# Seven-product layer: combinations kept in PSUM, products reordered, six weight chunks converted in layer 1, one GpSimd piece per tick

## The chip, the core and the metric

The kernel runs on one core of a Trainium2 chip. The metric is the device time of one execution in microseconds (us); lower is better. Engines are named as in the profile: PE (matmul), DVE (VectorE), ACT (ScalarE), POOL (GpSimd) and SP (the queue that issues DMAs).

## The reference

x has the shape 2 x 3008 x 256 in float32, so there are 6016 tokens of 256 numbers.

```python
X = np.fft.fft(np.fft.fft(x, axis=1), axis=2).real        # 2 x 3008 x 256
x = X.reshape(6016, 256)
h = x @ w_in                                              # 256 -> 2048
g = np.where(h > 0, h, np.exp(np.minimum(h, 0)) - 1)      # ELU
x = g @ w_out                                             # 2048 -> 256
h = x @ w2_in                                             # 256 -> 2048
g = np.maximum(h, 0) + alpha * np.minimum(h, 0)           # PReLU, alpha per column
return g @ w2_out                                         # 2048 -> 256
```

## The kernel before

**Arithmetic.** All matrix products are in float32r. An operand is split into hi (rounded by a copy on ACT) and lo = value - hi (a subtraction on POOL, sometimes on DVE), and a product is three matmuls: hi x hi, lo x hi, hi x lo (`PASSES`). The 6016 tokens lie in six blocks, each of two column sets of 512, 512, 480, 484, 512 and 512 tokens (`BLOCKS`). 2048 hidden columns are 16 tiles of 128 (`NFT`).

**Layer 1: 96 ticks.** `tick(t)` is one hidden tile of one block. Blocks 0 and 1 are interleaved in halves, the others run one after another; ticks 64 to 79 are block 4 and ticks 80 to 95 block 5. In a tick PE does gemm1 of t (6 matmuls, L413, into the two PSUM banks of the tag `mm`) and gemm2 of t-3 (12 matmuls, L429, into four accumulator banks `acc`). DVE forms pt and two ht from gemm1 (L546 to L548), ACT does relu and exp, DVE combines the ELU of t-1 (L515), ACT writes hi of t-2 (L525) and POOL lo of t-2 (two pieces, L531). gemm2 therefore waits for lo, and lo for hi. From tick 42 on (`E_PSUM`) the exp goes into the two PSUM banks of the tag `ee`.

**Side work in the ticks.** Hooks `pre`, `mid` and `end` of each tick carry work for layer 2. Its weights are stored as 64-bit numbers and are converted in halves of 512 columns: one ACT copy (`conv_y`, L307) and three integer steps on DVE (`conv_s`: L324, L326, L328). `KEEP` lists the chunks (("i" or "o", layer, chunk), tick of its load, of its first step, of its return) that are converted in layer 1 and parked in DRAM; `DIRECT` lists those converted in layer 2. For an "i" chunk `sums` makes sums of weight quarters and `split_sx` their hi and lo. `FINAL_1` splits parked chunks at ticks 84 to 94. `PREP_0` prepares block 0 for layer 2: `sub` makes differences of quarters (t3, t1, t2, t4; L484), `cast` their hi (ACT, L375) and lo (L376). When a block of layer 1 ends, `evac` copies its accumulators (DVE, L449, the first two, ACT the others).

**Layer 2: 48 pairs.** `pair(p)` does two hidden tiles of one block for both column sets, eight pairs for each block, by seven products of the Strassen kind in place of eight. A product is 3 matmuls (`product`, L602) with a weight quarter or sum (A11, A12, A22, S1 to S4) and a prepared operand (b11, t1, ...). They run into four PSUM banks: a and b of the tag `mm`, d and e of `ee`. Three banks take two products (a: A11 + A12, d: S1 + S4, e: S3 + A22), b takes S2. After them, `second(p-1)` does the 24 matmuls of gemm2 of the pair before (L429). The combinations are

```python
v  = A11 + S2          # P1 + P6            (L656, DVE)
h0 = d + v             # second column set  (L666, DVE)
h1 = (e + v, S1 + S3 + v)                 # (L668 and L652, L669, DVE)
```

with a itself the fourth. ACT does a relu of each (L665, L667, L670), DVE the PReLU (L673), ACT hi (`hi_2`, L620, 1024 wide, one for each hidden tile) and POOL lo (`lo_2`, L626, four pieces) for gemm2 in the next pair. In pairs 0 to 8 the rows of `FIRST` (one for each pair: what goes at its start, and after its products) carry the remaining weight conversion and the preparation of block 1; `AHEAD` carries the preparation of the later blocks. At the pair after a block ends (9, 17, 25, 33, 41) ACT and DVE also evacuate four accumulators.

The order on every engine is the order in which the code issues instructions (`manual_schedule`); each engine goes through its own in order.

Of the kernel before, what the change touches and what calls it, by code (L numbers as in the profile page):

```python
# [100 lines left out]
def tile_fft_moe_elu_moe_prelu(  # L101
# [254 lines left out]
    def w_split(kind, layer, c, i):  # L356
# [10 lines left out]
        act(out=hi, in_=v, func=ACTF.Copy)  # L367
        nc.gpsimd.tensor_tensor(out=lo, in0=v, in1=hi.bitcast(F32), op=ALU.subtract)


    sx = []
    s3 = {}

    def hi_lo(hi, lo, v, eng):
        act(out=hi, in_=v, func=ACTF.Copy)  # L375
        eng.tensor_tensor(out=lo, in0=v, in1=hi.bitcast(F32), op=ALU.subtract)  # L376

    def sums(c, eng, ks=(0, 1, 2, 3)):
# [4 lines left out]
        s = s3[c]
        ops = [(s[:, 1], w[:, 0, 0], w[:, 0, 1], ALU.subtract), (w[:, 0, 1], w[:, 0, 1], w[:, 1, 1], ALU.add),
               (s[:, 0], w[:, 0, 1], w[:, 0, 0], ALU.subtract), (s[:, 2], w[:, 1, 0], s[:, 0], ALU.subtract)]
        for k in ks:
            o, a, b, op = ops[k]
            eng.tensor_tensor(out=o, in0=a, in1=b, op=op)

    def split_sx(c, i):  # L390
# [87 lines left out]
    def sub(bl, name, eng=nc.vector):  # L478
# [5 lines left out]
        eng.tensor_tensor(out=o, in0=a, in1=b, op=ALU.subtract)  # L484
# [12 lines left out]
    def cast(bl, name, eng="g"):  # L497
# [131 lines left out]
    def pair(p, pre, mid, end):  # L629
        for fn in pre:  # L630
            fn()
        if p - 1 in pr:
            lo_2(p - 1, 0)
        if p < NP:
            bl, j = divmod(p, NFT // 2)
            n = BLOCKS[bl][2]
# [12 lines left out]
        if p < NP:
            e = tile_("ee")  # L650
            product(p, S3, "t3", e, True, False)
            tt(out=h1[:, 1], in0=e[:, 0:n], in1=h1[:, 1], op=ALU.add)  # L652
# [4 lines left out]
            product(p, A12, "b21", a, False, True)
            product(p, S4, "b22", d, False, True)
            product(p, A22, "t4", e, False, True)
        for fn in mid:  # L660
# [50 lines left out]
    with tc.manual_schedule():  # L711
# [54 lines left out]
        for bl, t in LOAD_ZB.items():  # L766
            at(t, load_zb, bl)
        for key, t_ld, t0, t_get in KEEP:
            at(t_ld, load, key)
# [8 lines left out]
            at(t_get, fetch_w, key)
        for t, kind, c, i in FINAL_1:
            at_split(t, kind, 2, c, i)  # L780
        for key, t in DIRECT.items():
            (at if t else at2)(t, load, key)

        def conv3(kind, c, i):
            for step in range(3):
# [9 lines left out]
            "sums": lambda c: sums(c, nc.vector),  # L795
            "sx": lambda c: [split_sx(c, i) for i in range(3)],
        }
        for p, (pre, mid) in enumerate(FIRST):
            for what, *args in pre + mid:
                where = "pre" if (what, *args) in pre else "mid"  # L800
                if p == 0:
                    at(NT - 1, does[what], *args, where="end")
                else:
                    at2(p - 1, does[what], *args, where=where)
# [5 lines left out]
        at(PREP_0[0], load_xs, 0, where="mid")  # L810
        for i, name in enumerate(("t3", "t1", "b11", "t2", "t4", "b21", "b22")):
            t = PREP_0[i + 1]
            if name[0] == "t":
                at(t, sub, 0, name, nc.gpsimd, where="end")
            if name != "t4":
                at(t + 1, cast, 0, name, where="mid")
        at(PREP_0[7] + 2, cast, 0, "t4", where="mid")
# [90 lines left out]
```

## Time and profile before

| | before |
|---|---|
| median of 3 runs | 985.65 us (985.25 to 987.08) |
| the profiled execution | 987.81 us |
| its span in the trace | 986.0 us |
| granted TensorE clock, mean over the span | 0.997 |
| PE busy | 955.3 us |
| DVE, ACT, POOL busy | 757.0, 650.9, 653.8 us |

The profiled execution is 1.81 us longer than its span and 2.16 us longer than the median. Layer 1's ticks 64 to 95 run from 341.00 to 479.44 us, layer 2's pairs from 479.44 us to the end.

### The profile page before, as it was taken

The page shows a single profiled execution, that of the slowest core. Times are in us where ns is not written, and L with a number is a line of the kernel's source. Part 1 is how long each engine was busy: PE and PEld are TensorE (multiplying, and loading weights), DVE is VectorE, ACT ScalarE, POOL GpSimd, SP SyncE. Part 2 cuts the span into 40 slices and gives each one's busy share as a digit, 9 for nine tenths or more (in the row PEclk, how much of TensorE's full clock was granted, in tenths as well). Part 3 has the DMA queues.
Part 4 walks back from the last instruction along what each step waited for, and adds up shares of the span by engine and source line. Part 5 has one row for each costly group of instructions (what it writes and reads, how often), then busy time and mean ns, then how long its engine had stood idle before and what let it go on. Part 6 is the DMA issues. An engine that isn't in the chain of part 4 may idle for free.

```text
span 986.0 us, 12143 instructions
## 1 busy us (share of the span) xinstructions
PE 955.3 (97%) x4206; PEld 770.0 (78%) x4206; DVE 757.0 (77%) x1002; ACT 650.9 (66%) x877; POOL 653.8 (66%) x492
## 2 busy tenths in 40 slices
PE   9799989999999999999999999999999999999998
PEld 3576757788888877778777778888888888888886
DVE  2797989989999989777899986676767576757554
ACT  5577776766788887788766655656555556556554
POOL 1365667766867867878777966666675675666553
PEclk9999999999999999999999999999999999999999
DMA  8963322201211311021230020002002002001001
GB/s 317 331 203 85 86 76 86 96 21 66 76 51 54 118 62 53 2 85 43 86 129 1 0 83 1 1 1 84 1 0 83 1 1 84 1 1 43 1 1 43
DMA packets 27109, 63.04 MB, mean 64 GB/s; under 512 B 3044, under 2 KB 12516, under 8 KB 25000
## 3 DMA queue, kind: packets, MB, share of 16 engines
q1 hardware_dynamic: 25632, 61.03, 18.9%
q10 hardware_dynamic: 1160, 1.07, 0.4%
q8 instruction: 33, 0.54, 0.2%
q0 software_dynamic: 256, 0.17, 0.1%
q14 instruction: 28, 0.23, 0.1%
HBM read 40.99 MB, written 21.27 MB: 63 GB/s over the span
## 4 chain that ended last, share of the span: by engine, by line
PE 73%; DVE 14%; ACT 5%; issue 3%; POOL 3%; DMA 2%; DVEq 0%; ACTq 0%; SPq 0%; POOLq 0%
PE acc L429 40%; PE eet L602 11%; PE mmt L602 8%; PE mmt L413 6%; POOL lo L531 2%; DVE pt L546 2%; DVE ht L548 2%; DVE et L673 2%; DVE et L518 1%; PE eet L182 1%; PE eet L413 1%; ACT et L565 1%; DVE sg L326 1%; ACT hi L525 1%; PE mmt L182 1%
## 5 line engine op out<-in xcount | busy, mean ns | idle before, releaser
L429 PE MATMUL acc<-hi,wo 128*128 128x512 f32 (+2 forms) x1536 | 470.9, 388 | 4.3 <-ACT hi L525 2.4
L626 POOL TENSOR_TENSOR lo<-et,hi 128x512 fp32r<-128x512 f32 (+2 forms) x190 | 255.3, 1367 | 160.6 <-ACT hi L620 154.9
L429 PEld LDWEIGHTS acc<-hi,wo 128*128 128x128 f32 x1536 | 289.1, 188 | 61.5 <-ACT hi L525 3.3
L531 POOL TENSOR_TENSOR lo<-et,hi 128x512 fp32r<-128x512 f32 (+2 forms) x192 | 268.8, 1424 | 93.9 <-ACT hi L525 62.3
L429 PE MATMUL acc<-lo,wo 128*128 128x512 f32 (+2 forms) x768 | 299.1, 390 | 9.5 <-POOL lo L531 9.5
L429 PEld LDWEIGHTS acc<-lo,wo 128*128 128x128 f32 x768 | 144.8, 189 | 43.8 <-POOL lo L531 16.0
L565 ACT ACTIVATE et<-ht 128x1024 f32<-128x1024 f32 (+3 forms) x97 | 100.2, 1033 | 87.4 <-DVE ht L548 76.8
L413 PE MATMUL mmt<-zt,wi 128*128 128x512 f32 (+2 forms) x462 | 121.1, 395 | 1.8 <-ACT zt L273 0.8
L652 DVE TENSOR_TENSOR ht<-eet,ht 128x512 f32<-128x512 f32 (+2 forms) x48 | 32.6, 679 | 113.9 <-ACT ht L645 113.9
L620 ACT ACTIVATE hi<-et 128x1024 fp32r<-128x1024 f32 (+2 forms) x96 | 99.9, 1040 | 23.6 <-DVE et L673 22.0
L673 DVE SCALAR_TENSOR_TENSOR et<-et,oma_sb,ht 128x512 f32<-128x512 f32 (+2 forms) x96 | 110.4, 1189 | 0.0
L413 PEld LDWEIGHTS mmt<-zt,wi 128*128 128x128 f32 x462 | 86.8, 189 | 23.3 <-issue 3.0
L525 ACT ACTIVATE hi<-et 128x1024 fp32r<-128x1024 f32 (+3 forms) x97 | 99.1, 1022 | 3.0 <-DVE et L518 2.5
L546 DVE SCALAR_TENSOR_TENSOR pt<-zb,an_sb,mmt 128x512 f32<-128x512 f32 (+2 forms) x77 | 56.2, 730 | 29.6 <-PE mmt L413 29.4
L641 ACT ACTIVATE p<-mmt 128x512 f32<-128x512 f32 (+2 forms) x48 | 28.3, 589 | 74.6 <-PE mmt L602 74.6
L670 ACT ACTIVATE et<-ht 128x1024 f32<-128x1024 f32 (+2 forms) x48 | 50.2, 1046 | 40.7 <-DVE ht L669 40.6
L518 DVE SCALAR_TENSOR_TENSOR et<-et,ht 128x1024 f32<-128x1024 f32 (+2 forms) x44 | 66.8, 1521 | 1.8 <-POOL lo L531 1.1
L602 PE MATMUL eet<-xo,wi 128*128 128x512 f32 (+2 forms) x216 | 60.8, 390 | 7.0 <-DVE ht L652 7.0
L515 DVE SCALAR_TENSOR_TENSOR et<-eet,ht 128x512 f32<-128x512 f32 (+2 forms) x106 | 66.5, 669 | 0.0
L602 PE MATMUL mmt<-xo,wi 128*128 128x512 f32 (+2 forms) x216 | 60.1, 386 | 0.9 <-ACT p L641 0.9
L572 ACT ACTIVATE eet<-et 128x512 f32<-128x512 f32 (+2 forms) x106 | 58.4, 584 | 3.4 <-DVE et L515 1.8
L602 PE MATMUL eet<-xo,sx 128*128 128x512 f32 (+2 forms) x216 | 60.0, 386 | 0.0
(125 smaller groups left out, 1330.0 us busy)
## 6 DMA issues: line engine op xcount, KB each, us to landing
w<-w_in SPq DMA_DIRECT2D x8, 1024.0 KB, 5.3
w<-w_out SPq DMA_DIRECT2D x8, 1024.0 KB, 8.0
vt<-ud SPq DMA_DIRECT2D x6, 1024.0 KB, 4.7
ud<-uc SPq DMA_DIRECT2D x20, 256.0 KB, 4.3
xd<-xs SPq DMA_DIRECT2D x8, 512.0 KB, 3.5
xs<-xd SPq DMA_DIRECT2D x4, 1024.0 KB, 10.6
out_t<-ot SPq DMA_DIRECT2D x16, 256.0 KB, 2.2
xc<-x SPq DMA_DIRECT2D x5, 768.0 KB, 7.9
```

What stands on the lines that cost most here:

```text
L413: mm(out=p[:, 0:n], lhsT=lhsT, rhs=rhs, start=(i == 0), stop=(i == len(ops) - 1))
L429: mm(out=accs[L, bl][d][t][:, 0:n], lhsT=w[:, a, o, d * 128:(d + 1) * 128], rhs=(hi, lo)[b][:, t, 0:n], start=(f == first and i == 0), sto ...
L515: stt(out=s["e"][:, i, :], in0=s["x"][i], scalar=-1.0, in1=s["h"][:, i, :], op0=ALU.add, op1=ALU.max)
L518: stt(out=s["e"][:, i], in0=s["e"][:, i], scalar=-1.0, in1=s["h"][:, i], op0=ALU.add, op1=ALU.max)
L525: act(out=s["hi"][:, i, 0:s["n"]], in_=s["e"][:, i], func=ACTF.Copy)
L531: nc.gpsimd.tensor_tensor(out=s["lo"][:, i, 0:n], in0=s["e"][:, i, :], in1=s["hi"][:, i, 0:n].bitcast(F32), op=ALU.subtract)
L546: stt(out=pt[:, 0:n], in0=zb[bl][:, 0:n], scalar=an_sb[:, f:f + 1], in1=p[0], op0=ALU.mult, op1=ALU.add)
L565: act(out=s["e"][:, i], in_=s["h"][:, i], func=ACTF.Relu, scale=-1.0)
L602: mm(out=bank[:, 0:n], lhsT=w[:, a], rhs=x2[b][:, 0:n], start=(first and m == 0), stop=(last and m == 2), skip_group_check=True)
L620: act(out=s["hi"][f][:, :, 0:n], in_=s["g"][f], func=ACTF.Copy)
L626: eng.tensor_tensor(out=s["lo"][f][:, t, 0:n], in0=s["g"][f][:, t], in1=s["hi"][f][:, t, 0:n].bitcast(F32), op=ALU.subtract)
L673: stt(out=o, in0=o, scalar=oma_sb[:, 2 * j + f:2 * j + f + 1], in1=h, op0=ALU.mult, op1=ALU.add)
```

## The change

**Pairs.** The products come in the order P1 (A11 into a), P6 (S2 into b), P5 (S1 into d), P7 (S3 into e), then A12, S4, A22 into a, d and e. DVE adds v = b + P1 into SBUF; all other combinations are written in place into PSUM: b = e + v, b += P5, d += v, e += v. Relu and PReLU work on the four banks singly (512 wide, one operand in PSUM). Both `hi_2` of a pair stand at its end, both `lo_2` at the start of the next.

**Weights.** `KEEP` has a sixth chunk, ("i", 2, 3); the six start every seven ticks and do their two halves in six ticks in a row. `FIRST` spreads the steps of the two chunks that stay in layer 2 as two per pair over pairs 1 to 6; the first conversion copy moves from the end of tick 95 into pair 0.

**POOL.** A helper `two` puts the hi of a split into `mid` of a tick (on ACT ahead of its relu) and the lo at the `end` on POOL, so that a tick holds at most one such piece, or one call of `sums`, beside the two of its own lo. The four `sub` of block 0 go from POOL to DVE (ticks 64, 66, 74, 78). `sub` of t3, t1 and t2 of block 1 go from DVE to POOL.

```diff
 KEEP = [
-    (("i", 2, 2), 63, 66, 95),
+    (("i", 2, 2), 59, 62, 95),
+    (("i", 2, 3), 66, 69, 98),
...
-PREP_0 = (64, 67, 70, 73, 76, 79, 82, 85)
+PREP_0 = [("x", 62), ("t3", 64, 65), ("t1", 66, 67), ("b11", None, 69), ("t2", 74, 75), ("b21", None, 76), ("t4", 78, 82),
...
 FIRST = [
-    ((("s", "o", 2, 0),), (("y", "o", 2, 1), ("w", "o", 1, 0), ("w", "o", 1, 1))),
+    ((("s", "o", 2, 0, 0), ("s", "o", 2, 0, 1)), (("y", "o", 2, 1), ("w", "i", 2, 0), ("w", "i", 2, 1))),
...
+    later = {}
+    def hi_lo(hi, lo, v, eng="g", key=None):
         act(out=hi, in_=v, func=ACTF.Copy)
-        eng.tensor_tensor(out=lo, in0=v, in1=hi.bitcast(F32), op=ALU.subtract)
+        fn = lambda: engine(eng).tensor_tensor(out=lo, in0=v, in1=hi.bitcast(F32), op=ALU.subtract)
+        if key:
+            later[key] = fn
+        else:
+            fn()
...
             lo_2(p - 1, 0)
+        if p - 1 in pr:
+            lo_2(p - 1, 1, nc.vector if p == NP else nc.gpsimd)
         if p < NP:
...
             product(p, A11, "b11", a, True, False)
             p1 = wk.tile([128, 512], F32, tag="zb", name="p1")
             act(out=p1[:, 0:n], in_=a[:, 0:n], func=ACTF.Copy)
-            h1 = wk.tile([128, 2, 512], F32, tag="h", name="ht")[:, :, 0:n]
-            d = tile_("ee")
-            product(p, S1, "t1", d, True, False)
-            act(out=h1[:, 1], in_=d[:, 0:n], func=ACTF.Copy)
-        if p - 1 in pr:
-            hi_2(p - 1, 1)
-            lo_2(p - 1, 1, nc.vector if p == NP else nc.gpsimd)
-        if p < NP:
-            e = tile_("ee")
-            product(p, S3, "t3", e, True, False)
-            tt(out=h1[:, 1], in0=e[:, 0:n], in1=h1[:, 1], op=ALU.add)
-            b = tile_("mm")
+            b = bank("mm")
             product(p, S2, "t2", b, True, True)
             v = wk.tile([128, 512], F32, tag="zb", name="v")
             tt(out=v[:, 0:n], in0=b[:, 0:n], in1=p1[:, 0:n], op=ALU.add)
+            d = bank("ee")
+            product(p, S1, "t1", d, True, False)
+            p5 = wk.tile([128, 2, 512], F32, tag="h", name="p5")[:, 0]
+            act(out=p5[:, 0:n], in_=d[:, 0:n], func=ACTF.Copy)
+            e = bank("ee")
+            product(p, S3, "t3", e, True, False)
+            a, b, d, e, v, p5 = (i[:, 0:n] for i in (a, b, d, e, v, p5))
+            tt(out=b, in0=e, in1=v, op=ALU.add)
             product(p, A12, "b21", a, False, True)
             product(p, S4, "b22", d, False, True)
             product(p, A22, "t4", e, False, True)
+            tt(out=b, in0=b, in1=p5, op=ALU.add)
...
-            act(out=g[0][:, 0], in_=a[:, 0:n], func=ACTF.Relu, scale=-1.0)
-            tt(out=h0, in0=d[:, 0:n], in1=v[:, 0:n], op=ALU.add)
-            act(out=g[0][:, 1], in_=h0, func=ACTF.Relu, scale=-1.0)
-            tt(out=h1[:, 0], in0=e[:, 0:n], in1=v[:, 0:n], op=ALU.add)
-            tt(out=h1[:, 1], in0=h1[:, 1], in1=v[:, 0:n], op=ALU.add)
-            act(out=g[1], in_=h1, func=ACTF.Relu, scale=-1.0)
+            tt(out=d, in0=d, in1=v, op=ALU.add)
+            tt(out=e, in0=e, in1=v, op=ALU.add)
+            outs = ((g[0][:, 0], a, 0), (g[1][:, 1], b, 1), (g[0][:, 1], d, 0), (g[1][:, 0], e, 1))
+            for o, h, f in outs:
+                act(out=o, in_=h, func=ACTF.Relu, scale=-1.0)
...
         if p in pr:
             hi_2(p, 0)
+            hi_2(p, 1)
...
+        def two(t, fn, *args):
+            key = (fn.__name__,) + args
+            at(t, lambda: fn(*args, key=key), where="mid")
+            at(t, lambda: later.pop(key)(), where="end")
...
-            for i, t in enumerate((t0, t0 + 4)):
+            for i, t in enumerate((t0, t0 + 3)):
                 at_conv(t, (t, t + 1, t + 2), *key, i)
...
-                at(t0 + 7, sums, key[2], nc.gpsimd, (0, 1), where="end")
-                at(t0 + 8, sums, key[2], nc.gpsimd, (2, 3), where="end")
+                at(t0 + 8, sums, key[2], "g", (0, 1), where="end")
+                at(t0 + 9, sums, key[2], "g", (2, 3), where="end")
                 for i in range(3):
-                    at(t0 + 9 + i, split_sx, key[2], i, where="end")
+                    two(t0 + 10 + i, split_sx, key[2], i)
```

**Places in the order.** On PE, the seven products of one pair (mmt is a or b, eet d or e; wi a weight quarter, sx a sum; xo and xr prepared operands), before:

```order
L602 MATMUL mmt<-xo,wi_4184 128x512 x3
L602 MATMUL eet<-xo,wi_4184 128x512 x3
L602 MATMUL eet<-xo,sx 128x512 x3
L602 MATMUL mmt<-xo,sx 128x512 x3
L602 MATMUL mmt<-xr,wi_4184 128x512 x3
L602 MATMUL eet<-xr,sx 128x512 x3
L602 MATMUL eet<-xr,wi_4184 128x512 x3
```

and of the change:

```order
L611 MATMUL mmt<-xo,wi_4201 128x512 x3
L611 MATMUL mmt<-xo,sx 128x512 x3
L611 MATMUL eet<-xo,wi_4201 128x512 x3
L611 MATMUL eet<-xo,sx 128x512 x3
L611 MATMUL mmt<-xr,wi_4201 128x512 x3
L611 MATMUL eet<-xr,sx 128x512 x3
L611 MATMUL eet<-xr,wi_4201 128x512 x3
```

The product into b has moved from the fourth place to the second, and those into d and e by one place back; the fifth, the second one into a, is where it was.

On ACT, the start of pair 9, the first pair of the second block (ot is the evacuation of the block before, p the copy of P1), before:

```order
L447 ACTIVATE ot<-acc_4498 128x512
L447 ACTIVATE ot<-acc_4500 128x512
L620 ACTIVATE hi<-et 128x1024
L641 ACTIVATE p_5165<-mmt 128x512
L645 ACTIVATE ht<-eet 128x512
L620 ACTIVATE hi<-et 128x1024
L665 ACTIVATE et<-mmt 128x512
```

and of the change:

```order
L456 ACTIVATE ot<-acc_4515 128x512
L456 ACTIVATE ot<-acc_4517 128x512
L629 ACTIVATE hi<-et 128x1024 x2
L652 ACTIVATE p_5183<-mmt 128x512
L660 ACTIVATE p_5195<-eet 128x512
L677 ACTIVATE et<-mmt 128x512 x2
L677 ACTIVATE et<-eet 128x512 x2
```

The second hi has moved ahead of the copy of P1.

On DVE, tick 66 (the last three rows up to the next pt are its end), before:

```order
L546 SCALAR_TENSOR_TENSOR pt<-zb,an_sb,mmt 128x512
L547 TENSOR_TENSOR ht<-pt,mmt 128x512
L548 TENSOR_TENSOR ht<-pt,mmt 128x512
L449 COPY xs<-acc_2495 128x484
L449 COPY xs<-acc_2497 128x484
L515 SCALAR_TENSOR_TENSOR et<-eet,ht 128x512 x2
L324 TENSOR_SCALAR sg<-w_2960 128x512
L546 SCALAR_TENSOR_TENSOR pt<-zb,an_sb,mmt 128x512
```

and of the change:

```order
L555 SCALAR_TENSOR_TENSOR pt<-zb,an_sb,mmt 128x512
L556 TENSOR_TENSOR ht<-pt,mmt 128x512
L557 TENSOR_TENSOR ht<-pt,mmt 128x512
L458 COPY xs<-acc_2500 128x484
L458 COPY xs<-acc_2502 128x484
L524 SCALAR_TENSOR_TENSOR et<-eet,ht 128x512 x2
L327 SCALAR_TENSOR_TENSOR sg<-w_2803,sg 128x512
L493 TENSOR_TENSOR xs<-xs 128x512
L555 SCALAR_TENSOR_TENSOR pt<-zb,an_sb,mmt 128x512
```

The tick now holds the subtraction for t1 (L493) besides a conversion step and the evacuation.

## Rows read from the trace of the kernel before

**Rows 1.** Page, busy time of each engine, with its share and instructions.

```profile
PE 955.3 (97%) x4206; PEld 770.0 (78%) x4206; DVE 757.0 (77%) x1002; ACT 650.9 (66%) x877; POOL 653.8 (66%) x492
```

**Rows 2.** PE's waits, 200 to 479 us: total us, times, longest us.

```profile
PE acc L429 <- POOL lo L531: 5.4, 7, 1.9
```

**Rows 3.** PE's waits, 479 to 600 us.

```profile
PE eet L602 <- DVE ht L652: 7.0, 6, 1.6
PE mmt L602 <- ACT p L641: 0.9, 1, 0.9
```

**Rows 4.** Timeline of PE (start, us): first product of pairs 0, 9, 10.

```profile
479.44 0.84 PE L602 MATMUL mmt<-xo,wi 128*128 128x512 f32 x3
...
584.96 0.84 PE L602 MATMUL mmt<-xo,wi 128*128 128x512 f32 x3
...
595.16 0.84 PE L602 MATMUL mmt<-xo,wi 128*128 128x512 f32 x3
```

**Rows 5.** Timeline of PE: gemm1 of ticks 62, 64, 71, 72, 95.

```profile
333.12 1.48 PE L413 MATMUL mmt<-zt,wi 128*128 128x484 f32 x6
...
341.00 1.55 PE L413 MATMUL mmt<-zt,wi 128*128 128x512 f32 x6
...
373.28 1.52 PE L413 MATMUL mmt<-zt,wi 128*128 128x512 f32 x6
...
377.36 1.52 PE L413 MATMUL mmt<-zt,wi 128*128 128x512 f32 x6
...
475.36 1.52 PE L413 MATMUL mmt<-zt,wi 128*128 128x512 f32 x6
```

**Rows 6.** Timeline of POOL in tick 68, with idle time before and its releaser.

```profile
360.05 1.29 POOL L484 TENSOR_TENSOR tx<-xs 128x512 f32<-128x512 f32 x1
362.08 1.82 POOL L376 TENSOR_TENSOR xo<-tx,xo 128x512 fp32r<-128x512 f32 x1 [0.74 <-ACT xo L375]
363.86 5.00 POOL L531 TENSOR_TENSOR lo<-et,hi 128x512 fp32r<-128x512 f32 x4
```

**Rows 7.** Window 360:400: busy us (x instructions) of PE, PEld, DVE, ACT, POOL; PEclk.

```profile
360.00:400.00 40.00, 37.70 (x158) 30.30 (x157) 32.17 (x49) 30.26 (x43) 33.26 (x29) 0.96 0.11 33
```

**Rows 8.** Timeline of DVE: a conversion step, then ticks 61 and 62.

```profile
330.03 1.08 DVE L328 SCALAR_TENSOR_TENSOR w<-w,sg 128x512 int32<-128x512 int32 x1
331.04 0.71 DVE L546 SCALAR_TENSOR_TENSOR pt<-zb,an_sb,mmt 128x484 f32<-128x484 f32 x1
...
332.42 0.65 DVE L548 TENSOR_TENSOR ht<-pt,mmt 128x484 f32<-128x484 f32 x1
...
334.13 0.71 DVE L546 SCALAR_TENSOR_TENSOR pt<-zb,an_sb,mmt 128x484 f32<-128x484 f32 x1
```

**Rows 9.** DVE groups by form, 240 to 400 us: busy us, mean ns; idle before.

```profile
L326 DVE SCALAR_TENSOR_TENSOR sg<-w,sg 128x512 int32<-128x512 int32 x9 | 10.5, 1164 | 0.0
L328 DVE SCALAR_TENSOR_TENSOR w<-w,sg 128x512 int32<-128x512 int32 x9 | 10.0, 1111 | 0.0
L324 DVE TENSOR_SCALAR sg<-w 128x512 int32<-128x512 int32 x9 | 7.4, 818 | 0.0
```

**Rows 10.** Line 484 on DVE: duration min/median/max in ns.

```profile
L484 DVE TENSOR_TENSOR tx<-xs x10: 645/678/1787, 520.6 to 863.1; 128x512 f32<-128x512 f32 x6, 128x480 f32<-128x480 f32 x2, 128x484 f32<-128x484 f32 x2
```

**Rows 11.** Timeline of ACT at the start of pair 9.

```profile
584.48 1.28 ACT L447 ACTIVATE ot<-acc 128x512 f32<-128x512 f32 x2 [2.11 <-PE acc L429]
585.65 1.05 ACT L620 ACTIVATE hi<-et 128x1024 fp32r<-128x1024 f32 x1
586.60 0.59 ACT L641 ACTIVATE p<-mmt 128x512 f32<-128x512 f32 x1
```

**Rows 12.** DVE groups by form, 600 to 640 us (four steady pairs).

```profile
L673 DVE SCALAR_TENSOR_TENSOR et<-et,oma_sb,ht 128x1024 f32<-128x1024 f32 x4 | 5.1, 1272 | 0.0
L669 DVE TENSOR_TENSOR ht<-ht,v 128x512 f32<-128x512 f32 x4 | 3.1, 770 | 0.0
L656 DVE TENSOR_TENSOR v<-mmt,p 128x512 f32<-128x512 f32 x4 | 2.8, 692 | 0.0
```

More of the change, by code (lines that the diff above doesn't have):

```diff
@@ L354, in load_an, with w_split @@
                           in_=ad[:, c * 512:(c + 1) * 512].rearrange("o (c p) -> (o p) c", p=128))
-    def w_split(kind, layer, c, i):
+    def w_split(kind, layer, c, i, key=None):
         t = w32[kind, layer, c]
@@ L366, in w_split, with engine @@
         v = t[:, i * 512:(i + 1) * 512]
-        act(out=hi, in_=v, func=ACTF.Copy)
-        nc.gpsimd.tensor_tensor(out=lo, in0=v, in1=hi.bitcast(F32), op=ALU.subtract)
+        hi_lo(hi, lo, v, key=key)
     sx = []
     s3 = {}
-    def hi_lo(hi, lo, v, eng):
+    def engine(e):
+        return {"v": nc.vector, "g": nc.gpsimd}[e]
+    later = {}
+    def hi_lo(hi, lo, v, eng="g", key=None):
         act(out=hi, in_=v, func=ACTF.Copy)
-        eng.tensor_tensor(out=lo, in0=v, in1=hi.bitcast(F32), op=ALU.subtract)
+        fn = lambda: engine(eng).tensor_tensor(out=lo, in0=v, in1=hi.bitcast(F32), op=ALU.subtract)
[3 more added lines that the diff above has]
+            fn()
     def sums(c, eng, ks=(0, 1, 2, 3)):
@@ L387, in sums, with split_sx @@
             o, a, b, op = ops[k]
-            eng.tensor_tensor(out=o, in0=a, in1=b, op=op)
-    def split_sx(c, i):
+            engine(eng).tensor_tensor(out=o, in0=a, in1=b, op=op)
+    def split_sx(c, i, key=None):
         if not sx:
@@ L476, in quarters, with sub @@
         return (xs[bl][:, k, t, 0:n] for k in range(2) for t in range(2))
-    def sub(bl, name, eng=nc.vector):
+    def sub(bl, name, eng="v"):
         b11, b12, b21, b22 = quarters(bl)
@@ L483, in sub @@
                    "t2": lambda: (tmp["t2"], b22, b12), "t4": lambda: (b12, b21, tmp["t2"])}[name]()
-        eng.tensor_tensor(out=o, in0=a, in1=b, op=ALU.subtract)
+        engine(eng).tensor_tensor(out=o, in0=a, in1=b, op=ALU.subtract)
     def operand(bl, name):
@@ L495, in operand, with cast @@
         return xo[bl][i][:, j, 0], xo[bl][i][:, j, 1]
-    def cast(bl, name, eng="g"):
+    def cast(bl, name, eng="g", key=None):
         n = BLOCKS[bl][2]
@@ L636, in pair @@
             n = BLOCKS[bl][2]
-            tile_ = lambda tag: ps.tile([128, 512], F32, tag=tag, name=f"{tag}t", bufs=2)
-            a = tile_("mm")
+            bank = lambda tag: ps.tile([128, 512], F32, tag=tag, name=f"{tag}t", bufs=2)
+            a = bank("mm")
             product(p, A11, "b11", a, True, False)
@@ L767, in tile_fft_moe_elu_moe_prelu @@
             at(t, load_zb, bl)
+        def two(t, fn, *args):
+            key = (fn.__name__,) + args
+            at(t, lambda: fn(*args, key=key), where="mid")
+            at(t, lambda: later.pop(key)(), where="end")
         for key, t_ld, t0, t_get in KEEP:
             at(t_ld, load, key)
-            for i, t in enumerate((t0, t0 + 4)):
+            for i, t in enumerate((t0, t0 + 3)):
                 at_conv(t, (t, t + 1, t + 2), *key, i)
             if key[0] == "i":
-                at(t0 + 7, sums, key[2], nc.gpsimd, (0, 1), where="end")
-                at(t0 + 8, sums, key[2], nc.gpsimd, (2, 3), where="end")
+                at(t0 + 8, sums, key[2], "g", (0, 1), where="end")
+                at(t0 + 9, sums, key[2], "g", (2, 3), where="end")
                 for i in range(3):
-                    at(t0 + 9 + i, split_sx, key[2], i, where="end")
-            at(t0 + 9, keep_w, key)
-            at(t_get, fetch_w, key)
+                    two(t0 + 10 + i, split_sx, key[2], i)
+            at(t0 + 10, keep_w, key)
+            (at if t_get < NT else at2)(t_get % NT, fetch_w, key)
         for t, kind, c, i in FINAL_1:
-            at_split(t, kind, 2, c, i)
+            two(t, w_split, kind, 2, c, i)
         for key, t in DIRECT.items():
             (at if t else at2)(t, load, key)
-        def conv3(kind, c, i):
-            for step in range(3):
-                conv_s(kind, 2, c, i, step)
         does = {
             "y": lambda kind, c, i: conv_y(kind, 2, c, i),
-            "s": conv3,
+            "s": lambda kind, c, i, step: conv_s(kind, 2, c, i, step),
             "w": lambda kind, c, i: w_split(kind, 2, c, i),
@@ L794, in tile_fft_moe_elu_moe_prelu @@
             "cast": cast,
-            "sums": lambda c: sums(c, nc.vector),
+            "sums": lambda c: sums(c, "g"),
             "sx": lambda c: [split_sx(c, i) for i in range(3)],
@@ L798, in tile_fft_moe_elu_moe_prelu @@
         for p, (pre, mid) in enumerate(FIRST):
[L799 to L804, printed above, removed]
+            for where, todo in (("pre", pre), ("mid", mid)):
+                for what, *args in todo:
+                    at2(p, does[what], *args, where=where)
         for bl in range(2, NBLK):
@@ L809, in tile_fft_moe_elu_moe_prelu @@
                         at2(bl * NFT // 2 - len(AHEAD) + i, does[what], bl, *args, where=where)
[L810 to L817, printed above, removed]
+        for name, t, *cs in PREP_0:
+            if name == "x":
+                at(t, load_xs, 0, where="mid")
+            else:
+                if t:
+                    at(t, sub, 0, name, "v", where="end")
+                two(cs[0], cast, 0, name, "g")
         for t in range(NT):
```

16 lines of the change are left out of this document (8 added, 8 removed), and 15 rows, old and new, of the table FIRST.

## The prediction

> **What bounds the kernel now.** I read the page first, then PE's waits by stretch, then the timelines where they lie. PE is busy 955.3 of 986.0 us [rows 1], so a change can only win PE's idle time or its slow clock; the number of matmuls stays. The pace of undisturbed work comes from starts of like work. Pair 9 to pair 10 is 595.16 - 584.96 = 10.20 us for 45 matmuls, or 0.2267 each [rows 4]; a tick of block 4 takes 377.36 - 373.28 = 4.08 us for 18, the same pace [rows 5]. Against it I measure the two stretches that the change touches.
>
> Ticks 64 to 95: 475.36 - 341.00 = 134.36 us for 31 ticks, at 4.08 each 126.48. **7.9 us are lost.** PE names one releaser in the whole of 200 to 479 us: POOL's lo, 5.4 us in seven waits, the longest 1.9 [rows 2]. The timeline of POOL shows why: in tick 68 it does a subtraction for block 0 (1.29), waits 0.74 for ACT, does a cast's lo (1.82), and only at 363.86 the lo that PE waits for [rows 6]. Behind this the granted clock is 0.96 in 360 to 400 us [rows 7]: 0.04 x 40 = 1.6 us of clock (a stretch at the lower level of 1.2 GHz). Waits and clock together make most of the 7.9; the rest is waits too short to be named.
>
> Pairs 0 to 8: 584.96 - 479.44 = 105.52 us. Pair 0 has no gemm2 of a pair before it but the last three ticks' gemm2 of layer 1, 21 + 36 = 57 matmuls; with 8 x 45 that is 417, at 0.2267 94.5 us. **11.0 us are lost.** Here PE waits 7.0 us in six places for DVE's L652, and 0.9 for P1's copy [rows 3]; L652 empties bank e before A22 may go on, and it stands behind conversion steps and blocks' differences on DVE. No pair after pair 8 names a wait: the steady pairs have nothing to win.
>
> **The change part by part.**
>
> *Layer 1, what is removed.* One piece per tick on POOL, with its hi made earlier in the tick, takes away the pile-up of [rows 6]: the subtraction (1.29) and the 0.74 go, and what is left beside the two lo pieces is one piece of 1.3 to 1.8, inside a tick of 4.08 with lo at 2.6. I take back all 7.9 us.
>
> *Layer 1, what is added: DVE.* A tick without a step occupies DVE for 334.13 - 331.04 = 3.09 us at 484 columns [rows 8], about 3.25 at 512, so 4.08 leaves 0.83. A step of 1.08 holds DVE from 330.03 to 331.04, 1.01, so three steps (0.82 + 1.16 + 1.11 = 3.09 in the mean [rows 9]) count about 2.8. The change puts twelve steps into ticks 62 to 74 without a rest tick, 11.2 us; three of block 0's differences, at 0.68 alone and up to 1.79 [rows 10], say 1.2 each, 3.6; and the two evacuation copies of tick 66, about 1.2 by the shortest DVE rows there (0.65 [rows 8]). That is 16.0 against 13 x 0.83 = 10.8 of room: 5.2 us late. DVE may lag before PE feels it: with pt started at 331.04, the second bank came free at 332.42 + 0.65 = 333.07, and the next tick's product, begun at 333.12 [rows 5], asks for that bank three matmuls later, at 333.80. About 0.7 more than that lag of about 1 us is free, so 1.6 of the 5.2. **I give back 3.6 us.** Bounds: with the differences at 0.68 it is 2.0, and with the steps at less than their mean, nothing (before, three such steps in every four ticks ran without any PE wait for DVE [rows 2]); with the differences at 1.79, 5.4, and a second dip of the clock like that of [rows 7] makes it 7.
>
> The price of those differences is where the Trainium skill speaks against the change. The row shows 645/678/1787 ns for one and the same operation [rows 10], so other work beside it can more than double it. "SBUF — State Buffer", section "Who interferes with whom", says that a DVE instruction with two SBUF inputs contends with a GpSimd instruction that reads SBUF, by an exclusive lock, while one with a single SBUF input does not. By it each moved difference would meet POOL's lo and take about 1.8, the upper bound above, not 1.2; the trace agrees that such values occur, but its median is 0.68.
>
> *Steady pairs.* The new order asks these of DVE, in us after the pair's start T: P6 is done at about 1.6 and v (0.69 [rows 12]) at 2.3; P5's copy then (0.6); b = e + v after P7, about 2.97 to 3.66. A22 writes e at 6 x 0.68 = 4.08, so there is about 0.4 to spare; S4 writes d at 3.40, and P5's copy ends at 2.9. No in-place add of DVE in PSUM exists in this trace. Nearest are an add with one operand in PSUM, 0.692, and one with both in SBUF, 0.770 [rows 12]; I take 0.69. Below: nothing excludes that it is quicker, but no PE wait is left to win. Above: the 1024-wide row's 1.27 [rows 12], which is 0.2 us more than the 1.06 that the spare allows, 0.2 for each pair. DVE's work per pair falls (a wide instruction with both operands in SBUF goes), POOL's and ACT's stays nearly as it was. So steady pairs stay at 10.20.
>
> *Pairs at a block's start.* Before, ACT does the last evacuations, one hi (585.65, 1.05) and at 586.60 P1's copy, which ends at 587.19 [rows 11], 2.2 us after the pair began at 584.96. Now the second hi stands ahead of it, as the order shows. It occupies ACT for 586.60 - 585.65 = 0.95, so the copy ends at about 3.2. A12, the fifth product as before, overwrites that bank at 4 x 0.68 = 2.72. New wait: 0.5 us, in pairs 1, 9, 17, 25, 33 and 41. **I give back 3.2 us.** Queued behind the copy are P5's copy and the relus, so the tail of the pair moves with it and nothing more is added. Below: 0, if the evacuations come 0.5 earlier; above: 1.0 each, 6.
>
> *Pairs 0 to 8.* Two steps per pair in place of three in a row and whole sums; DVE has over 2 us free in a pair, so the steps no longer stand ahead of the add that frees e. Three differences of block 1 go to POOL, which has 10.2 - 4 x 1.3, 5 us, free in a pair. I take back the 11.0 and leave 0.6 (pair 0's start, and the first cast of block 1, whose data are loaded only in pair 2). Bounds 0 and 3: three waits of the mean size of [rows 3], 7.0 / 6 = 1.2, rounded down. The first load of the sixth chunk in pair 2 goes through SP's queue ahead of block 1's; that is in the 0.6.
>
> *Costed at nothing:* keeping combinations in PSUM frees SBUF traffic for others and costs no bank (four before, four after); the DRAM parking of a sixth chunk is two transfers of 0.5 MB beside a DMA system that is nearly empty there (a share of 0.11 [rows 7]). If that cover were gone, the pair that needs the chunk would wait, some 2 us once.
>
> **The sum.** 7.9 + 11.0 = 18.9 won; 3.6 + 3.2 + 0.6 = 7.4 given back; 11.5 less. The profiled execution took 987.81, span 986.0 and 1.81 around it, so 976.3 by that execution, which was 2.16 above the median of 985.65. **I predict 974 us** for the median. By the bounds (0 to 7, 0 to 6, 0 to 3, half of each at once) its own range is 970 to 979.
>
> **The rivals.**
>
> *DVE is not late in layer 1.* Steps and differences take their shortest rows, no wait for DVE arises and POOL's are gone: 3.6 better, 970; with no wait at the blocks' starts either 967. For it: before, PE never waited for DVE in that stretch. Against it: there the steps had a rest tick in four. Chance 0.14.
>
> *DVE gets in POOL's way.* All four differences and the twelve steps (two SBUF inputs in eight of them) overlap POOL's pieces; each side blocks the other, POOL's lo is late again, PE stops for about 2 us and the clock falls as in [rows 7]. Of layer 1's 7.9 nothing is won, the 3.6 is still paid: 974 + 7.9 = 982, 984 with the dip. For it: 1.79 beside 0.68 [rows 10], and 1.82 for a POOL cast [rows 6]. Chance 0.16. "SBUF — State Buffer" of the Trainium skill, by the rule named above, would make this the likelier end.
>
> *Slower: the in-place adds.* b = e + v must end before A22. If an add that reads and writes PSUM takes more than 1.06 us (0.69 + 0.37), each 0.1 beyond it costs 0.1 x 48 = 4.8 us, and the 11.5 are gone at about 1.3 us. At the 1.27 of [rows 12] the time is 974 + 10 = 984, at 1.4 it is 990. For it: such an add appears nowhere in the trace, and it reads two values and writes into one memory. Against it: an operand in PSUM costs less than one in SBUF in all rows here. Chance 0.08, at 988 or above.
>
> *The change doesn't do what it says.* The waits for L652 turn into waits for b = e + v of the same length (DVE still does the steps in those pairs), and layer 1 nets 4: 983.5 to 986. Chance 0.07, half of it within the limit.
>
> **Chances and range.** The forecast holds 0.55. A measurement of this kernel can tell about 0.2%, 2 us, so faster means below 983.7. Faster: 0.55 + 0.14 + 0.14 + 0.04 = 0.87; same 0.05; slower 0.08. The range takes in the first rival at its best and the second without the dip: 968 to 982, which leaves out 0.08, 0.07 and part of the second.
>
> **What would show it.** Right: between 340 and 480 us the waits for POOL's lo are gone and some for DVE's ht or pt stand in ticks 66 to 75, 3 to 4 us in all; in pairs 0 to 8 under 1 us of waits; in six pairs a wait of PE for ACT's P1 copy of about 0.5; the in-place add at about 0.69; steady pairs at 10.20. Wrong: waits of A22 for DVE in steady pairs, a granted clock below 1.00 in 340 to 480, or pairs 0 to 8 still above 97 us.

## The result and the profile after

The changed kernel takes **977.91 us** in the median of three executions, against 986.37 for the kernel before beside it: the ratio of the means is 0.9916, with a 95% interval of 0.9897 to 0.9936. Four more executions gave 978.06, and a ratio of 0.9918 (0.9903 to 0.9932). The change makes the kernel faster by 8 us; 974 was forecast, 11.65 less than the median then known. A fourth execution of the changed kernel, the one that was profiled first, lasted 3390.64 us with matmuls of about 1.1 us each throughout, in place of 0.39, and one of a later version 3027.2 us; both are left out of the medians given here (with the first the median is 978.28), and everything below is read from a profile of the changed kernel at 978.29 us.

The page of the changed kernel, busy time of each engine, answers to [rows 1]:

```profile
PE 954.8 (98%) x4206; PEld 767.5 (79%) x4206; DVE 725.3 (74%) x1045; ACT 654.3 (67%) x925; POOL 624.4 (64%) x497
```

PE's work is the same to 0.5 us; the span, 976.4 us, is 9.6 us shorter. PE's waits in ticks 64 to 95 (341.5 to 475.5 us), which answer to [rows 2], then from 479 to 600 us, which answer to [rows 3], then from 600 us to the end (total us, times, longest us):

```profile
PE acc L438 <- ACT xs L456: 1.1, 1, 1.1
PE mmt L422 <- DVE ht L557: 0.6, 2, 0.4
...
PE mmt L611 <- ACT p L652: 0.7, 2, 0.3
...
PE mmt L611 <- ACT p L652: 1.3, 4, 0.3
```

The waits for POOL's lo and for the DVE add that empties bank e (L652) are gone. In their place stand three others: DVE and an evacuation on ACT in layer 1, and P1's copy on ACT in layer 2, six times, after 600 us too, where the kernel before had no wait at all. Where the time is won shows in starts of the same work on PE, against [rows 4, 5] (gemm1 of ticks 64 and 95, first product of pairs 0, 9, 10 and 11):

```profile
341.55 1.55 PE L422 MATMUL mmt<-zt,wi 128*128 128x512 f32 x6
...
471.43 1.52 PE L422 MATMUL mmt<-zt,wi 128*128 128x512 f32 x6
...
475.51 0.84 PE L611 MATMUL mmt<-xo,wi 128*128 128x512 f32 x3
...
571.14 0.84 PE L611 MATMUL mmt<-xo,wi 128*128 128x512 f32 x3
...
582.20 0.84 PE L611 MATMUL mmt<-xo,wi 128*128 128x512 f32 x3
...
592.40 0.84 PE L611 MATMUL mmt<-xo,wi 128*128 128x512 f32 x3
```

| stretch | undisturbed | before | after |
|---|---|---|---|
| start of tick 64 | | 341.00 | 341.55 |
| ticks 64 to 95 | 126.48 | 134.36 | 129.88 |
| pairs 0 to 8 | 94.5 | 105.52 | 95.63 |
| pair 9 | 10.20 | 10.20 | 11.06 |
| pair 10 | 10.20 | 10.20 | 10.20 |

The window of ticks 64 to 95, which answers to [rows 7] with the same columns, shows a granted clock (third number from the end) of 1.00; over these ticks it was 0.99 before:

```profile
341.55:471.43 129.88, 128.11 (x559) 103.89 (x558) 116.23 (x175) 110.05 (x151) 107.64 (x90) 1.00 0.14 47
```

### The profile page after: what moved, and what is told of

Read it like the earlier page. It is cut to its first block, busy times and chain, and to the rows that moved or that the text cites. A ratio compares the mean times of both kernels' runs of the same rounds, so it can differ in the third digit from the quotient of the medians.

```text
span 3388.7 us, 12247 instructions
## 1 busy us (share of the span) xinstructions
PE 3382.5 (100%) x4206; PEld 1785.1 (53%) x4206; DVE 697.2 (21%) x1045; ACT 669.8 (20%) x925; POOL 582.3 (17%) x497
## 4 chain that ended last, share of the span: by engine, by line
PE 100%; ACT 0%; DVE 0%; issue 0%
PE acc L438 55%; PE eet L611 14%; PE mmt L422 11%; PE mmt L611 10%; PE eet L422 3%; PE eet L183 2%; PE eet L343 1%; PE mmt L183 1%; PE mmt L265 1%; PE mmt L264 1%; PE eet L264 0%; PE mmt L343 0%; PE eet L265 0%; PE mmt L730 0%; PE eet L239 0%; PE mmt L215 0%
## 5 line engine op out<-in xcount | busy, mean ns | idle before, releaser
L438 PE MATMUL acc<-hi,wo 128*128 128x512 f32 (+2 forms) x1536 | 1448.3, 1083 | 0.0
L438 PEld LDWEIGHTS acc<-hi,wo 128*128 128x128 f32 x1536 | 654.1, 426 | 579.3 <-issue 574.3
L438 PE MATMUL acc<-lo,wo 128*128 128x512 f32 (+2 forms) x768 | 818.2, 1067 | 0.0
L438 PEld LDWEIGHTS acc<-lo,wo 128*128 128x128 f32 x768 | 330.0, 430 | 291.1 <-issue 288.5
L422 PE MATMUL mmt<-zt,wi 128*128 128x512 f32 (+2 forms) x462 | 405.0, 1102 | 0.7 <-ACT zt L274 0.7
L422 PEld LDWEIGHTS mmt<-zt,wi 128*128 128x128 f32 x462 | 197.0, 427 | 186.6 <-issue 185.1
L611 PE MATMUL eet<-xo,wi 128*128 128x512 f32 (+2 forms) x216 | 193.0, 1080 | 0.0
L611 PE MATMUL mmt<-xo,wi 128*128 128x512 f32 (+2 forms) x216 | 192.8, 1075 | 0.0
L611 PE MATMUL eet<-xo,sx 128*128 128x512 f32 (+2 forms) x216 | 192.6, 1077 | 0.0
L611 PE MATMUL mmt<-xo,sx 128*128 128x512 f32 (+2 forms) x144 | 128.3, 1075 | 0.0
```

The costliest lines, as they stand in the source:

```text
L422: mm(out=p[:, 0:n], lhsT=lhsT, rhs=rhs, start=(i == 0), stop=(i == len(ops) - 1))
L438: mm(out=accs[L, bl][d][t][:, 0:n], lhsT=w[:, a, o, d * 128:(d + 1) * 128], rhs=(hi, lo)[b][:, t, 0:n], start=(f == first and i == 0), sto ...
L611: mm(out=bank[:, 0:n], lhsT=w[:, a], rhs=x2[b][:, 0:n], start=(first and m == 0), stop=(last and m == 2), skip_group_check=True)
```

## The experiments

**The change in two halves.** The same changed kernel was run again with them, for its profile.

> The changed kernel once more, for a profile of an undisturbed execution; 978.3 us as timed before. My sum of the prediction (974) is 4.3 low. Theory A (DVE is later in layer 1 than costed): ticks 64 to 95 still lose 7 to 8 us against 4.08 each, with PE waits for DVE in ticks 62 to 76, and pairs 0 to 8 lose about 0.6. Theory B (the pairs are later than costed): ticks 64 to 95 lose 3.6 or less and pairs 0 to 8 still lose 4 to 5, or the six pairs at a block's start lose 1.0 each in place of 0.5.

Ticks 64 to 95 lose 3.4 us and pair 9 loses 0.86, so of the two theories B holds, in its second form and with 0.86 in place of 1.0: layer 1 came out as costed, the pairs at a block's start did not.

The first half takes the kernel before and puts in the whole function `pair` of the change, and nothing else of it:

```diff
-            product(p, S1, "t1", d, True, False)
+            product(p, S2, "t2", b, True, True)
...
-            hi_2(p - 1, 1)
...
+            hi_2(p, 1)
```

> The kernel before with the new pair alone (products' order, combinations in PSUM, both hi at the pair's end); weight schedule, piece order on GpSimd and differences as before. By my sum the new pair by itself costs 3.2 us at the block starts and takes away no wait of pairs 0 to 8, since the conversion steps still stand three in a row ahead of the add that frees a bank: 989 to 990 against 986.4. Rival: the combinations in PSUM are what freed pairs 0 to 8 (less work on DVE): 980 to 983.

It took 983.05 us, a ratio of 0.9971 (0.9961 to 0.9981): 2.8 us faster, where my sum said about 3 slower. The rival holds, at the upper end of its 980 to 983. Its waits of PE from 479 to 600 us, with the conversion steps still three in a row:

```profile
PE mmt L602 <- ACT p L643: 2.0, 4, 1.1
PE eet L602 <- DVE mmt L655: 1.3, 1, 1.3
```

Of [rows 3] the 7.0 us for L652 are down to 1.3, in pair 0. DVE's timeline from pair 2 to pair 3 of the kernel before, with a row of POOL beside it, shows what was late there:

```profile
505.31 1.51 DVE L324 TENSOR_SCALAR sg<-w 128x512 int32<-128x512 int32 x1
506.86 1.67 DVE L326 SCALAR_TENSOR_TENSOR sg<-w,sg 128x512 int32<-128x512 int32 x1
508.56 1.67 DVE L328 SCALAR_TENSOR_TENSOR w<-w,sg 128x512 int32<-128x512 int32 x1
510.15 0.68 DVE L652 TENSOR_TENSOR ht<-eet,ht 128x512 f32<-128x512 f32 x1
...
512.74 1.67 DVE L669 TENSOR_TENSOR ht<-ht,v 128x512 f32<-128x512 f32 x1
...
516.85 0.42 DVE L324 TENSOR_SCALAR sg<-w 128x512 int32<-128x512 int32 x1
...
506.50 6.11 POOL L626 TENSOR_TENSOR lo<-et,hi 128x512 fp32r<-128x512 f32 x4
```

and with the new pair alone, up to pair 4:

```profile
504.69 0.48 DVE L324 TENSOR_SCALAR sg<-w 128x512 int32<-128x512 int32 x1
505.21 0.70 DVE L326 SCALAR_TENSOR_TENSOR sg<-w,sg 128x512 int32<-128x512 int32 x1
505.94 1.67 DVE L328 SCALAR_TENSOR_TENSOR w<-w,sg 128x512 int32<-128x512 int32 x1
...
509.40 0.70 DVE L655 TENSOR_TENSOR mmt<-eet,v 128x512 f32<-128x512 f32 x1 [0.60 <-PE eet L602]
...
519.15 0.68 DVE L647 TENSOR_TENSOR v<-mmt,p 128x512 f32<-128x512 f32 x1
...
525.17 0.42 DVE L388 TENSOR_TENSOR s<-w 128x256 f32<-128x256 f32 x1
...
505.41 5.87 POOL L626 TENSOR_TENSOR lo<-et,hi 128x512 fp32r<-128x512 f32 x4 [0.52 <-ACT hi L620]
```

Before, the three steps took 510.15 - 505.31 = 4.84 us, and DVE's own work for the pair 516.85 - 510.15 = 6.70, with no idle time between; L669 took 1.67 where undisturbed ones take 0.77 [rows 12]. With the new pair the own work of pair 3 is 525.17 - 519.15 = 6.02, and the steps, begun earlier, are partly at 0.5 to 0.7. DVE has idle time in pair 2, and A22 finds its bank free. Integer steps of 1.67 beside 0.70, and adds of 1.67 beside 0.77, are instructions that read two operands from SBUF; the new pair's own read at least one from PSUM and none of them is lengthened in these rows. The slow ones run while POOL is at work (before, from 506.50 to 512.61 in the row shown, and on single pieces just ahead of it and behind it); the 0.70 at 505.21 began before POOL did, at 505.41. That is what "SBUF — State Buffer" of the Trainium skill, section "Who interferes with whom", states of DVE beside GpSimd, and the trace agrees. L324, a tensor_scalar, which the same section names among the operations that can contend, is lengthened too (0.42 and 1.51).

The second half is the changed kernel with the whole old `pair` put back; weights, hooks and pieces stay as changed:

```diff
+            product(p, S1, "t1", d, True, False)
-            product(p, S2, "t2", b, True, True)
...
+            hi_2(p - 1, 1)
...
-            hi_2(p, 1)
```

> The changed kernel with the old pair (products' order and combinations in SBUF, second hi in the next pair); the rest of the change kept. By my sum it wins what the schedule won and loses none at the block starts: 978.3 less 3.2, about 975. Rival: without the new pair the waits of pairs 0 to 8 stay, 981 to 985.

It took 976.58 us, 0.9905 (0.9890 to 0.9920): less than the whole change, as my sum said, though by 1.5 us and not by 3.2. Its waits of PE from 479 to 600 us:

```profile
PE eet L611 <- DVE ht L661: 2.5, 3, 0.9
```

They lie in pairs 3 to 5: two steps per pair are still too many there for the old pair. What each half does by itself shows in the same starts as in the table above, here of pairs 0 and 9 with the new pair alone, then with the rest alone:

```profile
479.56 0.84 PE L602 MATMUL mmt<-xo,wi 128*128 128x512 f32 x3
...
578.72 0.84 PE L602 MATMUL mmt<-xo,wi 128*128 128x512 f32 x3
...
475.01 0.84 PE L611 MATMUL mmt<-xo,wi 128*128 128x512 f32 x3
...
573.27 0.84 PE L611 MATMUL mmt<-xo,wi 128*128 128x512 f32 x3
```

| | ticks 64 to 95 | pairs 0 to 8 | pair 9 |
|---|---|---|---|
| kernel before | 134.36 | 105.52 | 10.20 |
| new pair alone | 134.37 | 99.16 | 11.01 |
| the rest alone | 129.93 | 98.26 | 10.20 |
| whole change | 129.88 | 95.63 | 11.06 |

All that is won in layer 1 comes from the rest of the change. In pairs 0 to 8 the new pair alone wins 6.4 us and the rest alone 7.3, of the 9.9 that both win. The new pair clears pairs 2 to 7 but not pair 0, which takes 15.89 us with it and 13.23 with the rest alone, where the conversion steps begin only in pair 1. The rest alone leaves about 1.1 in each of pairs 3 to 5. At each block's start the new pair costs 0.7 to 0.9. Its order of products, its combinations in PSUM and its two hi at the end were put in together, so no run shows how much of its gain the combinations make by themselves.

**The second hi.** First it goes behind P1's copy in the next pair, then behind P5's too:

```diff
             act(out=p1[:, 0:n], in_=a[:, 0:n], func=ACTF.Copy)
+            if p - 1 in pr:                               # hi2_after_p1
+                hi_2(p - 1, 1)
+                lo_2(p - 1, 1)
...
             act(out=p5[:, 0:n], in_=d[:, 0:n], func=ACTF.Copy)
+            if p - 1 in pr:                               # hi2_after_p5, in its place
+                hi_2(p - 1, 1)
+                lo_2(p - 1, 1)
...
             hi_2(p, 0)
-            hi_2(p, 1)
```

> The changed kernel with one row moved on ScalarE: the second hi of a pair goes back into the next pair, behind the copy of P1 (and its GpSimd pieces with it). If the copy of P1 behind two hi costs 0.5 us in the six pairs at a block's start, as I costed it, this gives 975; if that wait does not exist, 978.3; if the later hi makes gemm2 wait for GpSimd in every pair, over 980.

> The changed kernel with the second hi of a pair moved on ScalarE behind both copies, that of P1 and that of P5, of the next pair. Theory: the 0.8 us lost in each of the six pairs at a block's start comes only from copies that stand behind two hi and so free banks a and d late; with both ahead of the second hi the six pairs go back to 10.20 and the time is 978.1 - 6 x 0.8 = 973.2. Rival: what ScalarE evacuates at a block's start is late whatever stands behind it, and 0.3 to 0.45 stay in each: 975 to 976.

They took 975.75 (0.9894, 0.9878 to 0.9911) and **972.97** (0.9859, 0.9843 to 0.9876). ACT's timeline at the start of pair 9 of the changed kernel, which answers to [rows 11], with PE's and DVE's beside it:

```profile
571.84 2.00 ACT L629 ACTIVATE hi<-et 128x1024 fp32r<-128x1024 f32 x2
573.74 0.58 ACT L652 ACTIVATE p<-mmt 128x512 f32<-128x512 f32 x1
...
573.18 0.84 PE L611 MATMUL eet<-xo,sx 128*128 128x512 f32 x3
574.37 0.96 PE L611 MATMUL mmt<-xr,wi 128*128 128x512 f32 x3 [0.35 <-ACT p L652]
575.17 0.85 PE L611 MATMUL eet<-xr,sx 128*128 128x512 f32 x3
575.90 0.98 PE L611 MATMUL eet<-xr,wi 128*128 128x512 f32 x3
...
574.35 0.69 DVE L656 TENSOR_TENSOR v<-mmt,p 128x512 f32<-128x512 f32 x1 [3.68 <-ACT p L652]
575.15 0.70 DVE L664 TENSOR_TENSOR mmt<-eet,v 128x512 f32<-128x512 f32 x1
```

The fifth product should start 0.68 after the fourth, at 573.86; it starts at 574.37, 0.51 late, just behind P1's copy. Its second matmul starts 0.34 after its first where 0.23 is usual, 0.11 more. v waits for the same copy, so b = e + v ends on DVE only at 575.85, and A22, which overwrites e, starts at 575.90: 0.04 more, and again 0.11 at its second matmul. With smaller delays the pair ends 0.86 late. With P1's copy ahead of the second hi only, the wait moves to bank d, which P5's copy frees (in that kernel's pair 9, begun at 570.48), and the pair takes 10.65:

```profile
574.20 0.96 PE L611 MATMUL eet<-xr,sx 128*128 128x512 f32 x3 [0.15 <-ACT p L664]
```

With both copies ahead (571.22 and 571.82, the second hi at 572.32) the pair is undisturbed, 579.78 - 569.58 = 10.20, and no wait of PE is named after 479 us. The theory of that run holds:

```profile
571.22 0.59 ACT L653 ACTIVATE p<-mmt 128x512 f32<-128x512 f32 x1
571.82 0.60 ACT L661 ACTIVATE p<-eet 128x512 f32<-128x512 f32 x1
572.32 1.05 ACT L629 ACTIVATE hi<-et 128x1024 fp32r<-128x1024 f32 x1
```

By the medians the six pairs cost 978.06 - 972.97 = 5.1 us; by the starts of their products each loses between 0.73 (block 3, 484 columns) and 0.86, 4.8 in all.

**Layer 1's wait.** In the changed kernel tick 66 holds block 3's evacuation, a conversion step and the t1 difference, as the order of the change shows. DVE there (timeline), and PE's largest wait:

```profile
354.05 1.23 DVE L458 COPY xs<-acc 128x484 f32<-128x484 f32 x2
355.19 1.28 DVE L524 SCALAR_TENSOR_TENSOR et<-eet,ht 128x512 f32<-128x512 f32 x2
356.38 0.68 DVE L327 SCALAR_TENSOR_TENSOR sg<-w,sg 128x512 int32<-128x512 int32 x1
356.98 0.69 DVE L493 TENSOR_TENSOR xs<-xs 128x512 f32<-128x512 f32 x1
...
357.65 0.73 PE L438 MATMUL acc<-hi,wo 128*128 128x512 f32 x2 [1.10 <-ACT xs L456]
```

ACT's evacuation stands behind its exp, and the exp, which needs the `ee` banks, behind the combination on DVE at 355.19. Ahead of that stand the two evacuation copies and what DVE had not finished in the ticks before; the tick's own step and difference come behind it. First I moved DVE's side work out of that tick (on top of the mended hi):

```diff
-    (("i", 2, 2), 59, 62, 95),
+    (("i", 2, 2), 57, 60, 95),        # chunks 2 to 5 one or two ticks earlier
-("t1", 66, 67)
+("t1", 67, 68)
...
+                t0 += 2 * (key[2] == 2)   # the sums of that chunk stay where they were
```

> As hi2_after_p5, and VectorE's work moved away from tick 66, where the evacuation copies of block 3 stand: the conversion of the fifth chunk ends at tick 65 in place of 67 (chunks 2 to 5 start one or two ticks earlier), and the t1 difference goes from tick 66 to 67. Theory: VectorE's backlog at tick 66 is what delays ScalarE's evacuation, the 1.1 us wait of PE, and part of the 1.0 us for ht: 971.5 to 972.5. Rival: with chunks back to back the backlog only arises earlier, and nothing is won: 973 to 974.

It took 973.47 in the median of three (0.9865, 0.9849 to 0.9882), the same as without the move. The rival holds. PE's waits from 200 to 480 us, and the longest of them:

```profile
PE mmt L422 <- DVE ht L557: 1.5, 4, 0.4
PE acc L438 <- ACT xs L456: 1.4, 2, 1.0
...
358.69 0.73 PE L438 MATMUL acc<-hi,wo 128*128 128x512 f32 x2 [0.97 <-ACT xs L456]
```

The wait for the evacuation stays where it was, 0.97 in place of 1.10: by the order on DVE, what was taken out of tick 66 stood mostly behind the combination that matters. The 0.2 us for ht behind it is gone, and three waits of 0.3 to 0.4 have come earlier, in ticks 43, 51 and 66. Ticks 64 to 95 take 129.12 us in place of 129.93, and ticks 48 to 63 take 63.93 in place of 63.21.

Then the amount of DVE's work was cut, by giving POOL the four differences again (on the changed kernel, without the mended hi):

```diff
-                    at(t, sub, 0, name, "v", where="end")
+                    at(t, sub, 0, name, "g", where="end")
```

> The changed kernel with the four differences of block 0 back on GpSimd, at the same ticks. Theory: they cost VectorE 0.68 us each where it is behind anyway, and GpSimd has room for one piece more in a tick (two lo of 1.3 and one of 1.3 to 1.8 in 4.08): 977 to 978. Rival: one more piece on GpSimd makes lo late again as in the kernel before: 979 to 983.

It took 975.91 (0.9891, 0.9876 to 0.9905), a little under what theory said: 2.15 us less than the changed kernel by the medians, 1.53 by the two profiled executions (976.76 and 978.29). In ticks 64 to 95 no wait of PE that the trace names is left, and they take 128.48 us in place of 129.88; the 2.0 above the undisturbed 126.48 lie in delays too short to be named:

```profile
341.42:469.90 128.48, 128.26 (x559) 104.06 (x558) 113.42 (x171) 110.17 (x151) 113.21 (x94) 1.00 0.14 47
```

POOL is busy 113.21 us there, against 107.64 in the changed kernel and 106.24 in the kernel before, and no wait for its lo is named, unlike in [rows 2]. 1.4 of the 1.53 us between the two profiles are these ticks.

**Both put right.** The last version has the second hi behind both copies and the differences on POOL.

> The changed kernel with both rows that cost it put right at once: the second hi of a pair behind both copies of the next pair, and the four differences of block 0 on GpSimd. If the two gains do not touch each other: 973.0 (the first alone) less the 1.4 to 2.2 that the second won, about 971; if they share a wait, 972 to 973.

It took **971.50 us** (970.72 to 971.86 in five), a ratio of 0.9846 (0.9832 to 0.9861), 6.6 us less than the change as made. 972.97 - 971.50 is the 1.5 of ticks 64 to 95 (129.93 us with the second hi moved alone, 128.47 here): the gains add.

**The times of the kernel before.** The prediction took 2.16 us off the profiled execution to come to a median.

> The kernel before once more, for a second profile. Its 13 times beside the first runs lie in two groups, eight from 984.7 to 985.9 and five from 987.0 to 987.7, and the execution that the prediction rests on (987.81) is of the upper one. Theory: the upper group has the longer wait for GpSimd's lo at tick 66 and the slower clock behind it; an execution of 985.5 loses some 2 us less in ticks 64 to 79. Rival: the groups differ elsewhere or all over.

> The kernel before once more, to catch a profile of its lower group (984.7 to 986.2). If the groups differ by the wait of about 1.9 at tick 66 and the slower clock behind it, ticks 64 to 79 lose some 2 us less in a profile of the lower group than the 134.3 of both profiles so far; if not, the difference lies elsewhere.

> As before_b, a second try for a profile of the lower group of the kernel before.

The thirteen times fall seven to six, not eight to five. The three took 987.62, 987.23 and 987.15, all of the upper group, so no profile of the lower one was to be had. All four profiles of that kernel take the same in ticks 64 to 95 (134.36, 134.34, 134.35 and 134.43 us), so they don't show what an execution of 985 us has less. The changed kernel has no such groups: its seven executions lie between 977.73 and 978.65. That the upper group is the clock's dip behind the long wait fits this, but it was not shown.

## Why the prediction was right, and where it was off

The time lies within the range and near the forecast; by its own steps:

- **Layer 1, what is removed: right.** No wait for POOL's lo of [rows 2] is named any more, and the slower clock of [rows 7] is gone too, so the rival in which DVE gets in POOL's way did not come.
- **Layer 1, DVE's backlog: the size right by luck, its make-up not.** 3.6 us were given back; ticks 64 to 95 lose 3.4, and 0.55 more ahead of tick 64, 0.4 of it a wait for DVE's ht. The three differences of ticks 64 to 74 took 0.68 and not 1.2, 1.6 us less in all. POOL was idle beside them, so the rule of "SBUF — State Buffer" of the Trainium skill, section "Who interferes with whom", did not come into play there; beside POOL's lo the fourth, in tick 78, took 1.32. The twelve steps took 13.4 us of DVE and not the 12.4 of the means in [rows 9], and tick 68 has no step, though the sum had twelve without a rest tick. These errors nearly cancel. DVE's groups by form, 335 to 400 us, and the fourth difference:

```profile
L329 DVE SCALAR_TENSOR_TENSOR w<-w,sg 128x512 int32<-128x512 int32 x4 | 5.3, 1319 | 0.0
L327 DVE SCALAR_TENSOR_TENSOR sg<-w,sg 128x512 int32<-128x512 int32 x4 | 4.5, 1126 | 0.0
...
L325 DVE TENSOR_SCALAR sg<-w 128x512 int32<-128x512 int32 x4 | 3.6, 890 | 0.0
...
L493 DVE TENSOR_TENSOR tx<-xs 128x512 f32<-128x512 f32 x2 | 1.4, 678 | 0.0
...
406.18 1.32 DVE L493 TENSOR_TENSOR xs<-xs,tx 128x512 f32<-128x512 f32 x1
```

  The largest single wait, 1.1 us for an evacuation on ACT, had no term: I let DVE's lateness reach PE only by the gemm1 banks, and it came by the exp's banks and ACT.
- **Steady pairs: right.** They stay at 10.20, and the in-place adds take 0.70, by their group of 590 to 630 us:

```profile
L664 DVE TENSOR_TENSOR mmt<-eet,v 128x512 f32<-128x512 f32 x4 | 2.8, 699 | 2.5 <-PE eet L611 2.5
```

  The slower rival, which needed more than 1.06, falls with it.
- **Pairs at a block's start: the mechanism right, the size off.** The wait is the 0.51 that the sum had; what each pair loses is 0.73 to 0.86, 4.8 in place of 3.2 us. The step that failed is "the tail of the pair moves with it and nothing more is added": in pair 9, 0.11 came on top at the first product behind the wait and 0.15 at A22, since v stands behind the same copy, and A22 behind v.
- **Pairs 0 to 8: the sum right, the reason half of it.** The 11.0 us are down to 95.63 - 94.5 = 1.1, and the 0.8 of pair 1 belongs to the point above. I put it down to the steps' spreading and to differences that go to POOL, and costed the combinations in PSUM at nothing. The spread steps with the old pair do win 7.3 of the 9.9, pair 0 among them, but leave 2.5 us of waits; the new pair alone, with three steps in a row, ends the waits of pairs 2 to 7.
- **From the profiled execution to the median.** 987.81 to 978.29 is 9.5, forecast 11.5; the blocks' starts make 1.6 of that difference of 2, and the 0.55 ahead of tick 64 about the rest. The other 2 us of the miss are the 2.16 that I took off: the changed kernel's profiled execution is only 0.23 above its median. An offset between one kernel's executions was carried over to a kernel that does not have it; what it consists of stays open.

## What to carry to other kernels

When a copy is pushed back on an engine, follow everything that hangs on it, not only the nearest bank: here P1's copy freed a bank and fed an add that freed another, and moving one hi behind the copies won 5 us. Moving a piece of an engine's work to the next tick did not help where the wait hung on work ahead of it (973.47 against 972.97); giving the work to an engine with room did (1.4 us in the ticks concerned). And a change that wins nothing in the steady loop, where nothing waits, may still clear the stretch in which other work crowds the same engine: the new pair left the steady pairs at 10.20 us and won 6.4 us in pairs 0 to 8.

## What the runs showed of the hardware

A DVE add that reads one operand from PSUM and one from SBUF and writes PSUM took 0.70 us for 128 x 512, and the one that writes SBUF 0.69. The first integer step took 1.51 and 0.42 us in two pairs one after the other of the kernel before, and the second 1.67 there and 0.70 with the new pair alone. After the wait of PE in the six pairs at a block's start, the second matmul starts 0.32 to 0.34 us after the first in place of 0.22 to 0.23, so that a wait of 0.5 us costs 0.1 more than itself.
